# Two attention and MLP layers on one Trainium2 core: the head's loads spread over two queues, and half of layer one's key sum made by GpSimd and VectorE adds

## The chip, the cores and the metric

The kernel runs on one core of a Trainium2 chip. The core has five instruction streams: TensorE (PE in the profile; its weight loads are shown apart as PEld), VectorE (DVE), ScalarE (ACT), GpSimd (POOL) and SyncE (SP), which here only issues DMAs. ScalarE and GpSimd issue DMAs too. Each engine runs its own instructions strictly in the order in which the program gives them; engines wait for one another by semaphores.

The metric is the device time of one execution in microseconds (us); lower is better.

## The reference

Input `x` has 2048 tokens of width 512 in bf16. The same two steps are made twice, with the same weights:

```python
phi = lambda t: jnp.where(t > 0, t + 1, jnp.exp(t)) + 1e-6
# x = x + A(layernorm(x)):   32 heads of width 16
q, k, v = heads(y @ wqkv)
kv  = einsum("bhsd,bhse->bhde", phi(k), v)
z   = einsum("bhsd->bhd", phi(k))            # sum over all 2048 tokens
num = einsum("bhqd,bhde->bhqe", phi(q), kv)
den = einsum("bhqd,bhd->bhq", phi(q), z) + 1e-6
A   = merge(num / den) @ wo
# x = x + B(layernorm(x)):   F = 1792
B   = gelu(y @ w1 + b1) @ w2 + b2
```

So a layer is a linear attention, whose `kv` and `z` need every token of the layer before the first output token can be made, and an MLP. "Layer one" and "layer two" are the two passes. Names in the code have the layer as 0 or 1.

## The kernel before, in words

**Tiles.** The 2048 tokens are 16 tiles of 128 tokens; four tiles are a chunk. A name such as `K0_5` is the K projection of layer one, tile 5; `Q0_1_3` is a Q projection of chunk 1. Matrix products are in bf16 with up to 512 columns at a time.

**Layer one's attention, by tile.** `norm` makes the statistics (`stats`, line 775, and `aggr`, 777, on VectorE), adds eps (`veps`, 782), raises to the power -1/2 on GpSimd (`pow`, 784) and applies the result, on VectorE (803) or, with a further small GpSimd operation `nmr` (795), on ScalarE (798). Tile 3 of chunk 0 has its statistics on ScalarE instead (`sum` 766, `sq` 770). The normalised tile is transposed, by a DMA of SP's queue (`TA0_n`, line 812), or in chunk 0 by TensorE (`PTC0`, `PTC1`, `PTA0_2`, `PTA0_3`, line 825) with a ScalarE copy out of PSUM (`tc...`, line 835). Tiles 0 and 1 of chunk 0 are transposed centred only (`cen`, 789), so that they need not wait for the power; their K projection is scaled afterwards. Then come the K projection (`attn_k`, line 879; K0_0 is written in four parts of the contraction, `K0_0a` to `K0_0d`, in the order given by `ks0`), `phi` (exp on ScalarE 847, relu on ScalarE 858, or a form with max on VectorE 851 and 853, min and add on VectorE 860 and 864, some adds on GpSimd), and the product G = y^T phi(K), which is summed over the tiles in PSUM (`attn_g_held`, line 984). V itself is never made: G is multiplied by its weights later (`KV`, line 1034).

**The sum z.** Layer one makes it by chunks on TensorE: `Z0_c` is 16 matmuls with one output column (line 970), and VectorE adds the result to `zs` (`zs0_c`, 941). Layer two adds phi(K) of chunks 0 to 2 up in `zacc` (fp32, `za...`, line 958, on VectorE or GpSimd), splits the total into two bf16 parts (`zhi` 923, `zlo` 926), sums these over the partitions by eight one-column matmuls (`ZH`, lines 933 and 934) and adds them to `zs` (`zsh`), and makes only chunk 3 as `Z1_3`. From `zs` VectorE builds the block matrix `zb` (1040) for the denominators of chunk 0 (`D0_0_n`, line 1100, then ln and exp on ScalarE) and the diagonal `dz` (1045) for a row of sums (`ZR`, 1048), with which the other chunks' denominators are made token by token on GpSimd and VectorE (1077 to 1089).

**The rest.** After `KV`, `M` and the output projection `WO` (1123) comes the residual add (1128), the second norm, `W1` (1153) with GELU on ScalarE (1158), `W2` (1190) and the residual add (1196, in layer two 1200). The bias b2 is added to `x` ahead of that by a 128 x 512 add in fp32 (`b20_n`, `b21_n`, line 1139) on VectorE or GpSimd. Layer two's norm, K projection and sums follow tile by tile behind layer one's `W2`. The last tile is written in two parts (1176 to 1202).

**What sets the order.** Everything is written down in `CONF`: `LOADS` has the first DMAs with their queue and what they wait for; `ORDER` has every engine's instructions by name, in order; `PLACES` has the buffer slot of each tile and thereby which earlier user must be done; `WAY` says on which engine an operation runs. The code builds a graph of operations, `Settled` takes orders and places from `CONF`, `assign_waits` turns the dependences into semaphore waits, and `play` emits the instructions. There is no planner in the kernel; an operation starts when its engine has finished those ahead of it and its inputs have come.

**The head.** Before the first K projection, TensorE runs 15 warm-up matmuls on constants (line 749). The loads, in their order by queue: SP issues `x0` (tile 0, 128 KB), `x1` (tiles 1 to 3 of chunk 0, 384 KB), `wka`, `wkc` (a quarter of the K weights each, 128 KB), `xc1` (chunk 1, 512 KB, only when `x0` has landed), `wq`, `xc3`, two transposes and `xc2`; ScalarE issues `wkb` and `wkd` as soon as VectorE has set `onesm`. The weights `wv`, `wo`, `w1`, `w2` are loaded from GpSimd's queue later.

The orders around the start, before the change:

```
SP   x0 x1 wka wkc xc1 wq xc3 TA0_0 TA0_1 xc2 TA0_5 TA0_4 ...
ACT  wkb wkd sumA0_3 tcC0 sqA0_3 tcC1 reluk0_0 tcA0_2 expk0_0 tcA0_3 expk0_1 ...
DVE  ones statsA0_0 aggrA0_0 cenA0_0 statsA0_2 statsA0_1 aggrA0_2 aggrA0_1 cenA0_1 normA0_0 vepsA0_1 normA0_2 statsA0_5 normA0_3 ...
PE   warm0 warm8 warm2 warm6 PTC0 warm1 warm7 warm5 warm4 warm3 K0_0a K0_0b PTC1 K0_0c K0_0d PTA0_2 K0_1 PTA0_3 K0_2 K0_3 G0_0_0 ...
PE   ... G0_7_0 Q0_1_1 Z0_3 Q0_0_3 Z0_2 G0_8_0 G0_9_0 D0_0_2 ...
```

The functions that the diff touches, and what calls them:

Of the kernel before, what the change touches and what calls it, by code (L numbers as in the profile page):

```python
# [1359 lines left out]
```

## Time and profile before

| | us |
|---|---|
| median of three runs | 323.17 |
| lowest, highest | 322.78, 323.90 |
| the profiled execution's own time | 323.1 |
| its span in the trace | 321.9 |
| TensorE busy | 318.0 |
| VectorE busy | 218.1 |
| ScalarE busy | 189.3 |
| GpSimd busy | 145.5 |

The profile page gives the busy time of each engine and its number of instructions, then the span in 40 equal slices with the busy share of each slice in tenths. "Chain" is the work that ended last, followed back from the end to what released each step. A group row has line, engine, operation, output and inputs, the number of instructions, then busy time and the mean length of one in ns, then the idle time of that engine just ahead of them and what ended it. A timeline row has start, length, engine, line and operation, and in brackets the idle time ahead of it with its releaser. A windows row has, for a stretch of time, the busy time of PE, PEld, VectorE, ScalarE and GpSimd with their instruction counts, the clock that TensorE was granted (1.00 is full), the mean share in which the 16 DMA engines were busy, and GB/s. Merged rows (x8) run from the start of the first to the end of the last; matmuls overlap, so the length of one row is not its cost on the engine: from start to start a 512-column matmul takes 0.216 us where nothing waits.

### The profile page before, as it was taken

To read this page: it belongs to the slowest core of one execution; us is meant where nothing else is said; L and a number is where in the kernel's file an instruction comes from. 1 tells how busy PE (TensorE), PEld (TensorE's weight loads), DVE (VectorE), ACT (ScalarE), POOL (GpSimd) and SP (SyncE) were. 2 spreads that over 40 slices of the span, in tenths; PEclk is the share of its full clock that TensorE was granted. 3 is DMA by queue.
4 is the path that set the end of the run, shared out by engine and by line. 5 is a ranking of instruction groups with operands and counts; after the bars stand their busy time and mean duration, and the time that the engine had idled before them with its cause. 6 is when DMAs were issued, how large, how long until landed. Compare 5 with 4: busy or idle time off the path is not lost.

```text
span 321.9 us, 4748 instructions
## 1 busy us (share of the span) xinstructions
PE 318.0 (99%) x1703; PEld 157.4 (49%) x1703; DVE 218.1 (68%) x529; ACT 189.3 (59%) x324; POOL 145.5 (45%) x216
## 2 busy tenths in 40 slices
PE   8999999999999999999999999999999999999997
PEld 3444554666444444444444444558544444444444
DVE  5998789999786774028848899999889881101103
ACT  5898656797730636667962367979634442663320
POOL 6573978688655355101822415887454163000000
DMA  7844793142121412111010200122232322201002
GB/s 257 200 81 85 241 348 85 35 82 36 33 49 34 82 33 51 34 33 32 18 40 10 51 16 0 35 51 52 50 62 54 98 65 67 49 0 35 16 33 65
DMA packets 52355, 21.68 MB, mean 67 GB/s; under 512 B 47532, under 2 KB 50860, under 8 KB 52332
## 3 DMA queue, kind: packets, MB, share of 16 engines
q1 hardware_dynamic: 50844, 16.37, 22.4%
q0 software_dynamic: 1056, 4.72, 4.3%
q10 hardware_dynamic: 432, 0.30, 0.3%
q8 instruction: 13, 0.21, 0.3%
q14 instruction: 10, 0.08, 0.1%
HBM read 8.00 MB, written 2.10 MB: 31 GB/s over the span
## 4 chain that ended last, share of the span: by engine, by line
PE 97%; DMA 2%; DVE 0%; issue 0%
PE ps L1153 30%; PE ps L1190 29%; PE ps L1123 9%; PE ps L879 8%; PE ps L896 6%; PE ps L984 4%; PE ps L1013 4%; DMA t<-in_A_x_dram 2%; PE ps L909 2%; PE ps L1176 1%; PE ps L970 1%; PE ps L1034 1%; PE ps L1057 1%; PE ps L1100 1%; DVE stats L775 0%; PE ps L1048 0%
## 5 line engine op out<-in xcount | busy, mean ns | idle before, releaser
L1158 ACT ACTIVATE gT<-ps,b1c 128x512 bf16<-128x512 f32 (+1 forms) x140 | 77.0, 601 | 68.7 <-PE ps L1153 68.1
L1153 PE MATMUL ps<-t,w 128*128 128x512 bf16 (+1 forms) x560 | 102.5, 336 | 0.0
L1190 PE MATMUL ps<-w,gT 128*128 128x512 bf16 x434 | 98.6, 379 | 0.0
L1153 PEld LDWEIGHTS ps<-t,w 128*128 128x128 bf16 x560 | 54.8, 98 | 43.7 <-ACT gT L1158 0.2
L1190 PEld LDWEIGHTS ps<-w,gT 128*128 128x128 bf16 x434 | 42.5, 98 | 50.4
L784 POOL TENSOR_TENSOR rstd<-veps,neghalf 128x1 f32<-128x1 f32 x64 | 39.0, 625 | 41.1 <-DVE veps L782 38.9
L847 ACT ACTIVATE eb<-ps 128x512 bf16<-128x512 f32 x62 | 35.4, 606 | 19.3 <-PE ps L896 7.3
L1200 DVE TENSOR_TENSOR yb<-ps,xsb 128x512 bf16<-128x512 f32 x15 | 10.2, 688 | 41.4 <-PE ps L1190 41.4
L775 DVE BATCH_NORM_STATS2 stats<-xsb 128x6 f32<-128x512 f32 x48 | 32.0, 681 | 0.3
L1123 PE MATMUL ps<-gtb,t 128*128 128x512 bf16 x128 | 31.4, 379 | 0.0
L879 PE MATMUL ps<-wqkv,t 128*128 128x512 bf16 x128 | 30.9, 379 | 0.3 <-ACT t L835 0.3
L858 ACT ACTIVATE rb<-ps 128x512 bf16<-128x512 f32 x43 | 25.3, 607 | 5.8 <-PE ps L879 5.8
L798 ACT ACTIVATE yb<-xsb,nmr,rstd 128x512 bf16<-128x512 f32 x21 | 16.9, 814 | 15.1 <-POOL nmr L795 15.1
L896 PE MATMUL ps<-wqkv,t 128*128 128x512 bf16 x96 | 24.1, 379 | 0.0
L1089 POOL TENSOR_TENSOR t<-t,rr 128x512 bf16<-128x512 bf16 x18 | 19.3, 1072 | 9.0 <-DVE rr L1085 6.4
L782 POOL TENSOR_SCALAR veps<-mv 128x1 f32<-128x1 f32 x35 | 8.2, 236 | 32.7 <-DVE mv L777 31.3
L1196 DVE TENSOR_TENSOR xsb<-ps,xsb 128x512 f32<-128x512 f32 x16 | 10.8, 678 | 17.9 <-PE ps L1190 17.9
L1139 POOL TENSOR_TENSOR xsb<-xsb,b2b 128x512 f32<-128x512 f32 x17 | 21.4, 1267 | 3.0 <-DVE yb L803 2.9
L1077 POOL TENSOR_TENSOR lr<-t,zrow 128x512 f32<-128x512 bf16 x14 | 16.5, 1179 | 7.3 <-ACT zrow L997 4.5
L1123 PEld LDWEIGHTS ps<-gtb,t 128*128 128x128 bf16 x128 | 12.5, 98 | 14.5
L803 DVE TENSOR_SCALAR yb<-xsb,mv,rstd 128x512 bf16<-128x512 f32 x27 | 14.5, 542 | 7.3 <-POOL rstd L784 6.0
L879 PEld LDWEIGHTS ps<-wqkv,t 128*128 128x128 bf16 x128 | 12.1, 98 | 14.7 <-ACT t L835 0.9
(99 smaller groups left out, 363.7 us busy)
## 6 DMA issues: line engine op xcount, KB each, us to landing
w<-in_B_w_dram POOLq DMA_DIRECT2D x4, 896.0 KB, 9.1
out_dram<-yb SPq DMA_DIRECT2D x15, 128.0 KB, 2.0
t<-in_A_x_dram SPq DMA_DIRECT2D x3, 512.0 KB, 4.8
t<-yb SPq DMA_TRANSPOSE x62, 2.5
wqkv<-in_A_wqkv_dram SPq DMA_DIRECT2D x1, 512.0 KB, 5.9
wqkv<-in_A_wqkv_dram POOLq DMA_DIRECT2D x1, 512.0 KB, 4.7
wo<-in_A_wo_dram POOLq DMA_DIRECT2D x1, 512.0 KB, 5.3
t<-in_A_x_dram SPq DMA_DIRECT2D x1, 384.0 KB, 3.3
```

The lines of the kernel that those rows point to most:

```text
L775: G.op("dve", lambda e: e.bn_stats(stats[:, s.slot, :], src()), 620, reads=src_keys, writes=[k + "s"], tiles=[s, *src_tiles], name=f"stats ...
L784: G.op("pool", lambda e: e.tensor_tensor(rstd[:, s.slot:s.slot + 1], veps[:, s.slot:s.slot + 1], neghalf[:], op=ALU.pow), 570, reads=[k + ...
L847: G.op("act", lambda e: e.activation(eb[:, et.slot, :], bank(bt), ACT.Exp, scale=by()), 478, reads=[src_key, *more_keys], writes=[f"e{tag} ...
L858: G.op("act", lambda e: e.activation(rb[:, rt.slot, :], bank(bt), ACT.Relu, scale=by()), 478, reads=[src_key, *more_keys], writes=[f"r{tag ...
L879: ins = e.matmul(bank(b), lhsT=yTa(yT)[:, dt, k * P:(k + 1) * P], rhs=wqkv[:, dt, D:2 * D], start=(i == 0 and n == 0), stop=(i == len(part ...
L896: ins = e.matmul(bank(b), lhsT=yTa(yT)[:, dt, k * P:(k + 1) * P], rhs=wqkv[:, dt, 0:D], start=(dt == 0), stop=(dt == DT - 1))
L1089: lambda e, d=d, tok=tok, heads=heads: e.tensor_tensor(heads(tok()), heads(tok()), rr[:, d.slot, :].unsqueeze(2).broadcast_to([P, H, DH]), ...
L1123: ins = e.matmul(bank(wb), lhsT=yTa(pq)[:, kt, k * P:(k + 1) * P], rhs=gtb[:, kt, :], start=(kt == 0), stop=(kt == DT - 1))
L1139: G.op("pool" if on_pool else "dve", lambda e: e.tensor_tensor(xsb[:, st, :], xsb[:, st, :], b2b[:], op=ALU.add), 1120 if on_pool else 600 ...
L1153: ins = e.matmul(bank(b, n), lhsT=w1[:, dt, ft * P:(ft + 1) * P], rhs=yTa(yT)[:, dt, k0 * P:k1 * P], start=(dt == 0), stop=(dt == DT - 1))
L1158: G.op("act", lambda e, ft=ft, b=b, k0=k0, k1=k1, n=n: e.activation(gT[:, g.slot, ft * 512 + k0 * P:ft * 512 + k1 * P], bank(b, n), ACT.Ge ...
L1190: ins = e.matmul(bank(b), lhsT=gT[:, g.slot, ft * 512 + k * P:ft * 512 + (k + 1) * P], rhs=w2[:, ft, :], start=(ft == 0), stop=(ft == FT - 1))
```

## The change

The change has three parts, and all orders are drawn anew with them.

1. `LOADS`: `x1` goes from the second place on SP's queue to the first on ScalarE's, behind the setting of `onesm`; `wkb` and `wkd` follow it there; `wka` and `wkc` move up on SP. The parts of K0_0 are taken in the order 0, 2, 1, 3.
2. `WAY["zc0"] = "0 1"`: in layer one, phi(K) of the eight tiles of chunks 0 and 1 is added up in `zacc` by seven adds (`zaA1`, `zaA3` to `zaA7` on GpSimd, `zaA2` on VectorE), and `zhiA`, `zloA`, `ZHA` and `zshA` take the total to `zs`, as layer two has it; `Z0_0`, `Z0_1` with their adds `zs0_0`, `zs0_1` go. `Z0_2` and `Z0_3` stay. The code for it was there already, unused in layer one.
3. `ORDER`, `PLACES` and other entries of `WAY` are new: in sum 14 of the b2 adds go from GpSimd to VectorE and two the other way, and some adds and products of layer two and of the denominators change engine.

The order in which chunks are taken (`CHUNKS`) can now be given, but it is 0, 1, 2, 3 in all three places as before; code for loading half a tile and for denominators half by token is added and not used.

```diff
-    LOADS=[['x0', 'sp', 'x', 0, 0, 1, ''], ['x1', 'sp', 'x', 0, 1, 4, ''], ['wkb', 'act', 'wk', 0, 2, 3, 'ones'], ['wka', 'sp', 'wk', 0, 0, 1, ''], ['wkd', 'act', 'wk', 0, 3, 4, ''], ['wkc', 'sp', 'wk', 0, 1, 2, ''], ['xc1', 'sp', 'x', 1, 0, 4, 'x0'], ['wq', 'sp', 'wq', 0, 0, 4, ''], ['xc3', 'sp', 'x', 3, 0, 4, ''], ['xc2', 'sp', 'x', 2, 0, 4, '']],
+    LOADS=[['x0', 'sp', 'x', 0, 0, 1, ''], ['wka', 'sp', 'wk', 0, 0, 1, ''], ['wkc', 'sp', 'wk', 0, 1, 2, ''], ['x1', 'act', 'x', 0, 1, 4, 'ones'], ['wkb', 'act', 'wk', 0, 2, 3, ''], ['wkd', 'act', 'wk', 0, 3, 4, ''], ['xc1', 'sp', 'x', 1, 0, 4, 'x0'], ['wq', 'sp', 'wq', 0, 0, 4, ''], ['xc3', 'sp', 'x', 3, 0, 4, ''], ['xc2', 'sp', 'x', 2, 0, 4, '']],
+    CHUNKS=[[0, 1, 2, 3], [0, 1, 2, 3], [0, 1, 2, 3]],
...
-        "den0_3": "tok", "den1_1": "tok", "den1_2": "tok", "den1_3": "tok", "ks0": "2|0|3|1", "normA0_0": "dve",
+        "den0_3": "tok", "den1_1": "tok", "den1_2": "tok", "den1_3": "tok", "ks0": "0|2|1|3", "normA0_0": "dve",
...
+        "za8": "dve", "za9": "dve", "zaA2": "dve", "zc0": "0 1",
...
-        def attn_z(L, c, pks):
-
-            by_sum = [int(v) for v in (eng("zc0") or "").split()] if L == 0 else list(range(NC - 1))
+        def attn_z(L, c, pks, order):
+
+            by_sum = [int(v) for v in (eng("zc0") or "").split()] if L == 0 else order[:NC - 1]
+            others = [v for v in order if v not in by_sum]
...
-            total(b, f"zc{L}_{c}", f"zs{L}_{c}", bool(L) or c != min(v for v in range(NC) if v not in by_sum))
-            if L == 0 and by_sum and c == max(v for v in range(NC) if v not in by_sum):
+            total(b, f"zc{L}_{c}", f"zs{L}_{c}", bool(L) or c != others[0])
+            if L == 0 and by_sum and c == others[-1]:
                 fold(True)
```

The orders around the places that the change touches, after it:

```
SP   x0 wka wkc xc1 wq xc3 TA0_1 TA0_0 xc2 TA0_4 TA0_7 ...
ACT  x1 wkb wkd sumA0_3 tcC0 sqA0_3 tcC1 expk0_0 tcA0_2 reluk0_0 tcA0_3 expk0_1 ...
DVE  ones statsA0_0 aggrA0_0 cenA0_0 statsA0_2 aggrA0_2 statsA0_1 aggrA0_1 vepsA0_1 cenA0_1 normA0_0 normA0_2 normA0_1 statsA0_4 normA0_3 ...
DVE  ... phik0_15 mink0_10 zhiA mink0_8 phik0_13 phik0_10 mink0_9 mink0_11 phik0_9 phik0_11 zloA zs0_2 zs0_3 zshA zb0 dz0 ...
POOL ... powA0_7 nmrA0_7 zaA1 vepsA0_5 powA0_5 ... powA0_14 nmrA0_15 zaA3 powA0_12 zaA4 nmrA0_14 vepsA0_10 powA0_10 nmrA0_10 vepsA0_8 zaA5 powA0_8 vepsA0_11 nmrA0_8 vepsA0_9 powA0_11 nmrA0_11 powA0_9 zaA6 zaA7 phik0_14 phik0_8 b1z wv wo w1_0 w1_1 ...
PE   warm0 warm7 warm4 warm3 warm6 PTC0 warm1 warm8 warm2 K0_0a warm5 K0_0b K0_0c PTC1 K0_0d PTA0_2 K0_1 PTA0_3 K0_2 K0_3 G0_0_0 ...
PE   ... K0_9 Q0_0_3 G0_7_0 Z0_3 G0_8_0 Z0_2 Q0_1_1 ZHA G0_9_0 D0_0_2 G0_10_0 ZR0 D0_0_0 ...
```

More of the change, by code (lines that the diff above doesn't have):

```diff
@@ L709, in load_w, with load_half @@
                                [f"{which}_{d}" for d in range(d0, d1)], name=name, kb=128 * (d1 - d0), after=after)
+        def load_half(name, queue, h, after):
+            G.parts[("x0", 0)] = (("x0", 0, 0), ("x0", 0, 1))
+            ps_ = slice(64 * h, 64 * h + 64)
+            loaded[name] = dma(queue, lambda e: e.dma_start(
+                t4[ps_, x0[0].slot, 0:D].rearrange("p (k d) -> p k d", k=1), rows(x_dram, 0)[ps_, 0:1, :]),
+                [("x0", 0, h)], [x0[0]], name=name, kb=64, after=after)
         for name, queue, what, at, lo, hi, behind in cf["LOADS"]:
             after = [loaded[b] for b in behind.split()]
-            if what == "x":
+            if what == "half":
+                load_half(name, queue, at, after)
+            elif what == "x":
                 load_x(name, queue, at, lo, hi, after)
@@ L887, in attn_q, with fn @@
         def attn_q(L, c, yT, pq):
-            if by_token(L, c):
-                for k in range(4):
+            half = by_half(L, c)
+            own = pq
+            if half:
+                own = tokq[(L, c)] = Tile(T4, f"pqt{L}_{c}")
+            n = 2 * P if half else 4 * P
+            if not by_token(L, c):
+                for kt in range(DT):
+                    b = Tile(psum, f"q{L}_{c}_{kt}" + "c" * half, "q")
+                    def fn(e, kt=kt, b=b):
+                        for dt in range(DT):
+                            ins = e.matmul(bank(b, n), lhsT=wqkv[:, dt, kt * P:(kt + 1) * P], rhs=yTa(yT)[:, dt, 0:n],
+                                           start=(dt == 0), stop=(dt == DT - 1))
+                        return ins
+                    G.op("pe", fn, 4 * MM if n == D else 4 * (n / 2.4 + 2.5), reads=[f"yT{L}_{4 * c + k}" for k in range(n // P)] + ["wq"], writes=[f"q{L}_{c}_{kt}" + "c" * half],
+                         tiles=[b, yT], name=f"Q{L}_{c}_{kt}" + "c" * half, lat=MM_DRAIN, n=4)
+                    phi(b, f"q{L}_{c}_{kt}" + "c" * half, lambda kt=kt: yTa(pq)[:, kt, 0:n], f"pq{L}_{c}_{kt}" + "c" * half, [pq], f"q{L}_{c}_{kt}" + "c" * half, n=n)
+            for k in range(4):
+                if by_token(L, c, k):
                     b = Tile(psum, f"q{L}_{c}_{k}", "q")
@@ L1042, in attn_kv @@
                  reads=["zs", "bdmask"], writes=["zb"], name=f"zb{L}", lat=40, fast=True)
-            if any(by_token(L, c) for c in range(NC)):
+            if any(by_token(L, c, 3) for c in range(NC)):
                 zr = Tile(psum, f"zr{L}", "t")
@@ new lines, in attn_den @@
+            half = by_half(L, c)
+            src = tokq[(L, c)] if half else pq
+            pt = pq if half or not by_token(L, c) else Tile(T4, f"pt{L}_{c}")
+            n = 2 * P if half else 4 * P
+            if not by_token(L, c):
+                for kt in range(DT):
+                    tag = f"{L}_{c}_{kt}" + "c" * half
+                    b = Tile(psum, f"d{tag}", "n")
+                    r = Tile(LR, f"lr{tag}")
+                    key = f"pq{L}_{c}_{kt}" + "c" * half
+                    G.op("pe", lambda e, kt=kt, b=b: e.matmul(bank(b, n), lhsT=zb[:, kt * P:(kt + 1) * P], rhs=yTa(pq)[:, kt, 0:n], start=True, stop=True),
+                         MM if n == D else n / 2.4 + 2.5, reads=[key, "zb"], writes=[f"d{tag}"], tiles=[b, pq], name=f"D{tag}", lat=MM_DRAIN)
+                    G.op("act", lambda e, b=b, r=r: e.activation(lr[:, r.slot, 0:n], bank(b, n), ACT.Ln, bias=eps6[:]), 575 if n == D else 362,
+                         reads=[f"d{tag}", "eps6"], writes=[f"l{tag}"], tiles=[b, r], name=f"ln{tag}", lat=90, table="exp")
+                    G.op("act", lambda e, r=r: e.activation(lr[:, r.slot, 0:n], lr[:, r.slot, 0:n], ACT.Exp, scale=-1.0), 536 if n == D else 323,
+                         reads=[f"l{tag}"], writes=[f"l{tag}"], tiles=[r], name=f"rec{tag}", lat=110, table="exp")
@@ L1093, in attn_den @@
[L1093 to L1105 removed]
+                         lambda e, kt=kt, r=r: e.tensor_tensor(yTa(pq)[:, kt, 0:n], yTa(pq)[:, kt, 0:n], lr[:, r.slot, 0:n], op=ALU.mult),
@@ new lines, in attn_den, with attn_out @@
+                     1150 if on_pool else 600, reads=[f"rr{tag}", f"pq{tag}"], writes=[f"pq{tag}"], tiles=[d, src],
+                     name=f"pr{tag}", lat=60, fast=not on_pool)
+                dma("sp", lambda e, k=k, tok=tok: e.dma_start_transpose(yTa(pt)[:, :, k * P:(k + 1) * P], tok()), [f"pt{tag}"],
+                    tiles=[src, pt], reads=[f"pq{tag}"], name=f"TP{tag}", sem=("pT", src, k), transpose=True)
+            return pt
+        def attn_out(L, c, k, pq, base, base_keys, base_tiles, first):
@@ L1116, in attn_out @@
             st = 4 * c + k
             wb = Tile(psum, f"wo{L}_{st}", "w")
-            parts = [(kt,) for kt in range(DT)] if st == 0 else [tuple(range(DT))]
+            parts = [(kt,) for kt in range(DT)] if first else [tuple(range(DT))]
             for part in parts:
@@ L1252, in build_kernel @@
         for L in range(2):
-            nxt = []
-            for c in range(NC):
+            nxt = {}
+            chunks = orders[1 + L]
+            for c in chunks:
                 yT = Tile(T4, f"yBT{L}_{c}")
```

155 lines of the change are left out of this document (66 added, 89 removed), and 471 rows, old and new, of tables (ORDER, PLACES, WAY).

## The prediction

> **What bounds the kernel now.** I read the page's busy shares and slices first, then the groups of TensorE (PE), the start of the timeline, and the windows of the stages that the change touches.
>
> ```profile
> span 321.9 us, 4748 instructions
> PE 318.0 (99%) x1703; PEld 157.4 (49%) x1703; DVE 218.1 (68%) x529; ACT 189.3 (59%) x324; POOL 145.5 (45%) x216
> PE   8999999999999999999999999999999999999997
> PE 97%; DMA 2%; DVE 0%; issue 0%
> L879 PE MATMUL ps<-wqkv,t 128*128 128x512 bf16 x128 | 30.9, 379 | 0.3 <-ACT t L835 0.3
> L1153 PE MATMUL ps<-t,w 128*128 128x512 bf16 (+1 forms) x560 | 102.5, 336 | 0.0
> L1190 PE MATMUL ps<-w,gT 128*128 128x512 bf16 x434 | 98.6, 379 | 0.0
> ```
>
> PE is busy in every slice, its work is 97% of the chain that ended last, and its large groups have no idle time before them. So only three things can move the time: how many matmuls there are, the head in which PE still waits, and a new wait. The other engines matter only where they become late for PE.
>
> **The head.** Rows of the timeline, from its start:
>
> ```profile
> 0.79 0.87 SPq L702 DMA_DIRECT2D t<-in_A_x_dram  x2
> 0.83 3.63 PE L749 MATMUL ps<-const-bfloat16-1.0 128*128 128x512 bf16 x10 [0.83 <-PEq L1345]
> 1.48 0.86 ACTq L708 DMA_DIRECT2D wqkv<-in_A_wqkv_dram  x2
> 4.60 0.63 ACT L766 ACTIVATE eb<-t 128x512 bf16<-128x512 bf16 x1 [2.52 <-DMA t<-in_A_x_dram]
> 5.23 0.58 ACT L835 ACTIVATE t<-ps 128x512 bf16<-128x512 bf16 x1
> 5.86 0.60 PE L879 MATMUL ps<-wqkv,t 128*128 128x512 bf16 x2 [0.30 <-ACT t L835]
> 6.73 0.14 DVE L782 TENSOR_SCALAR veps<-mv 128x1 f32<-128x1 f32 x1
> 6.98 0.60 ACT L835 ACTIVATE t<-ps 128x512 bf16<-128x512 bf16 x1 [0.47 <-PE ps L825]
> 7.48 0.68 ACT L858 ACTIVATE rb<-ps,rstd 128x512 bf16<-128x512 f32 x1
> 8.05 0.60 ACT L835 ACTIVATE t<-ps 128x512 bf16<-128x512 bf16 x1
> 8.09 0.69 DVE L775 BATCH_NORM_STATS2 stats<-t 128x6 f32<-128x512 bf16 x1 [0.72 <-DMA t<-in_A_x_dram]
> 8.53 0.70 ACT L847 ACTIVATE eb<-ps,rstd 128x512 bf16<-128x512 f32 x1
> 9.16 0.40 PE L825 MATMUL ps<-idp,yb 128*128 128x128 bf16 x4 [0.47 <-DVE yb L803]
> 9.39 1.89 PE L879 MATMUL ps<-wqkv,t 128*128 128x512 bf16 x8
> 9.59 0.60 ACT L835 ACTIVATE t<-ps 128x512 bf16<-128x512 bf16 x1 [0.37 <-PE ps L825]
> 10.09 0.68 ACT L847 ACTIVATE eb<-ps,rstd 128x512 bf16<-128x512 f32 x1
> 4.00:5.00 1.00, 0.85 (x9) 0.51 (x8) 0.91 (x3) 0.40 (x1) 0.66 (x2) 1.00 1.01 351
> 10.00:30.00 20.00, 20.00 (x122) 9.30 (x121) 18.35 (x60) 18.59 (x35) 11.56 (x30) 1.00 0.51 107
> ```
>
> Tiles 1 to 3 of chunk 0 (x1) have landed at 4.60, and ScalarE's sum of tile 3 starts at once (L766). ScalarE's order puts that sum ahead of the copy of the transposed tile 0 (5.23), which starts K0_0 (5.86). PE's last gap ends at 9.16. The copy of tile 3 at 9.59 lets K0_3 start behind K0_2 in the eight matmuls from 9.39: at 9.39 + 4 x 0.216 = 10.25 (a matmul of 512 columns is 0.216 us behind the one before: 1.89 less the last one's 0.38, over seven). The last two rows are of the windows (PE, weight load, VectorE, ScalarE, GpSimd, granted clock, DMA share, GB/s): the 16 engines of the DMA are full at 351 GB/s, and PE has no gap between 10 and 30 us. What K0_3 loses is lost to the end.
>
> **1. Sums on PE: -0.60 us.** A sum of phi(K) over one chunk is 16 one-column matmuls (L970); the change drops two such groups in layer one and adds ZHA, eight of the kind that layer two has already (L933, L934).
>
> ```profile
> 18.03 0.54 PE L970 MATMUL ps<-onesm,pkb 128*128 128x1 bf16 x16
> 18.43 0.81 PE L984 MATMUL ps<-pkb,yb 128*128 128x512 bf16 x3
> 189.24 0.17 PE L933 MATMUL ps<-onesm,dz 128*128 128x1 bf16 x1
> 189.44 1.89 PE L1013 MATMUL ps<-pkb,yb 128*128 128x512 bf16 x8
> ```
>
> A group costs 18.43 - 18.03 = 0.40, ZH 189.44 - 189.24 = 0.20: 0.20 - 2 x 0.40 = -0.60.
>
> **2. Loads: +0.29 us.** x1 is now the first load of ScalarE's queue, at 1.48 instead of second on SP, which is at 0.79 + 0.87/2 = 1.23: 0.25 later. SP sends wka (128 KB) in the place that x1 had; if its 131 KB go ahead of x1, that is 131/351 = 0.37 us more. Between 0.25 and 0.62, and, if wka and wkc both go first, 0.25 + 0.75 = 1.00. I take 0.45, since the two requests leave the queues a quarter of a microsecond apart and share the engines from then on. The sum of tile 3, the copy of tile 0 and K0_0 move by as much, to 6.31.
>
> Then VectorE's order: the centred tile 1 now stands behind the statistics of both tiles and one more small operation (0.14, the row at 6.73), and the two aggregates no longer run back to back; I take 0.33 of delay, bounds 0.14 and 0.5. The copy of tile 1 starts at 6.98 + 0.45 + 0.33 = 7.76. On ScalarE follow exp, the copy of tile 2, relu and the copy of tile 3, where before one of the two activations came behind it. From start to start the rows give copy 0.50 (6.98 to 7.48), relu 0.57 (7.48 to 8.05), copy 0.48 (8.05 to 8.53), and exp as relu, 0.57: 7.76 + 0.50 + 0.57 + 0.48 + 0.57 = 9.88 for the copy of tile 3. Before it was 9.59, with K0_3 0.66 behind; now K0_3 is at 10.54, +0.29. The other arm, by which chunk 1 lands (8.09), its statistics, tile 3's normalisation and its transpose (9.16), stays as it is: the same bytes are ahead of chunk 1, and one VectorE statistic (tile 4 for tile 5) is still ahead of the normalisation. So the term is not under 0, unless chunk 1 lands earlier too (-0.14, where ScalarE would have let K0_3 go without any delay of x1: 10.54 - 0.45 = 10.09 against 10.25). At x1 late by 1.00 it is +0.84.
>
> wkb and wkd go out behind x1; the last of them is wanted by K0_0d, right ahead of K0_1, which waits for the copy of tile 1 until about 8.4. The new part order of K0_0 (0, 2, 1, 3 for 2, 0, 3, 1) follows the new order of landing and is covered by the same copy. The fifteen warm-up matmuls are the same; one more of them lies ahead of the first transpose, under the 0.6 us that the copy waits anyway.
>
> **3. The denominator's start: +0.26 us.** ZHA gives zs, zs gives zb (VectorE), zb lets D0_0_2 (L1100) go. Before:
>
> ```profile
> 36.91 1.89 PE L984 MATMUL ps<-pkb,yb 128*128 128x512 bf16 x8
> 37.08 0.36 DVE L941 TENSOR_TENSOR zs<-ps,zs 128x4 f32<-128x4 f32 x2 [0.77 <-PE ps L970]
> 37.48 0.69 DVE L1040 TENSOR_TENSOR zb<-bdmask,zs 128x512 bf16<-128x512 bf16 x1
> 38.63 0.38 PE L1100 MATMUL ps<-t,zb 128*128 128x512 bf16 x1
> ```
>
> The last sum matmul started 0.03 before the G products, at 36.88; two adds and zb took until 38.17, and D0_0_2 came at 38.63, behind two G products: 0.46 to spare. Now one G product (4 x 0.216 = 0.86) stands between ZHA and D0_0_2. From the last matmul of ZHA: 0.16 for its result (the length of the L934 kind's row of 189.24), 0.04, 0.20 for the single add, 0.04, 0.69 for zb, about 1.15; PE comes after 0.03 + 0.86 = 0.89. Stall 0.26. With the two adds' time it is 1.29 - 0.89 = 0.40; if the G product is held up itself, nothing: 0 to 0.4.
>
> **4. Adds: 0, up to +2.3.** The eight tiles of phi(K) become seven adds into zacc, six on GpSimd and one on VectorE, then a copy and a subtraction on VectorE.
>
> ```profile
> L958 POOL TENSOR_TENSOR zacc<-zacc,pkb x4: 1156/1158/1337, 157.5 to 179.4; 128x512 f32<-128x512 f32 x4
> L923 DVE TENSOR_SCALAR dz<-zacc x1: 421/421/421, 183.4 to 183.4; 128x512 bf16<-128x512 f32 x1
> L926 DVE TENSOR_TENSOR eb<-zacc,dz x1: 684/684/684, 185.6 to 185.6; 128x512 bf16<-128x512 f32 x1
> 31.42 1.15 POOL L864 TENSOR_TENSOR pkb<-eb,rb 128x512 bf16<-128x512 bf16 x1 [4.94 <-DVE eb L860]
> L1139 POOL TENSOR_TENSOR xsb<-xsb,b2b x17: 1149/1159/1681, 70.3 to 266.4; 128x512 f32<-128x512 f32 x17
> L1139 DVE TENSOR_TENSOR xsb<-xsb,b2b x15: 672/684/1370, 79.3 to 277.2; 128x512 f32<-128x512 f32 x15
> L1034 PE MATMUL ps<-gtb,wqkv x32: 219/219/219, 46.6 to 203.0; 128*128 128x128 bf16 x32
> ```
>
> Six adds of 1.158 are 6.95 us. GpSimd has 11.56 of 20 us busy from 10 to 30, so 18.5 of 20, and it stood idle for 4.94 us before its phi(K) at 31.42. The powers and means of the norms of chunks 2 and 3 stand in order behind the adds; followed through by these durations the last power ends near 28.4 and its tile is transposed by 32.1, when PE wants it. Cover: that 4.94 us. If it is gone, each late add delays all K projections behind it by 1.16. VectorE gets 0.69 + 0.42 + 0.68 + 0.2 less two adds of 0.18, some +1.6, in a stretch in which it was busy 18.35 of 20; its remaining 1.65 us are the cover, and zloA and zb come at its end.
>
> **5. The rest: 0.** The weight loads on GpSimd's queue now go out behind both of its phi(K) products (the one at 31.42 and the next) instead of between them; the first of them, Wv, is needed only at 46.6 (L1034). Sixteen b2 adds change engine, 14 to VectorE (0.684 each, 1.16 on GpSimd); they are done any time before their residual add, and VectorE has 32% free over the span. What stands behind one of them in order waits 0.68 at most, if that cover is missing.
>
> **Sum.** The profiled execution took 323.1 (1.2 beside its span of 321.9; the median of three is 323.17, 322.78 to 323.9): 323.1 - 0.60 + 0.29 + 0.26 + 0 = 323.05, say 323.1. Its own range, by the ends of terms 2 and 3, is 322.5 to 323.7. Some 0.3%, 1 us, is what a measurement of this kernel can tell from no change.
>
> **Rivals.** (a) Slower: GpSimd becomes late in layer one. It decides once the last power ends later than 28.4. For it: 18.5 of 20 us, and the same adds on it took up to 1.681 where VectorE's took up to 1.370 against 0.684, so the two engines stretch each other at times. With all six adds at 1.681 GpSimd's stretch holds 11.56 + 10.1 = 21.6 of 20 us: 1.6 late, 324.7. One add late gives 324.3, two 325.4. Against it: most of its operations there are small and wait for VectorE anyway. The Trainium skill ("SBUF — State Buffer", Who interferes with whom) says that the port pair which VectorE and GpSimd share is an exclusive lock, held for a whole instruction; by that rule the stretched rows are the cost to expect, and it speaks against moving adds to GpSimd beside a busy VectorE. The maxima of the L1139 rows agree, the medians do not.
>
> (b) Slower: VectorE's extra b2 adds make PE's later tiles late, one or two by 0.7 to 1.4 us: 324.0 to 324.5. Against it: PE's 0.0 idle at L1153 and L1190.
>
> (c) Slower: PE idles longer in the head, its clock drops again. The ten first warm-ups (4352 columns by their order) took 3.63 us, half the 0.216 us per 512 later; some 3 us at that rate cost 1.5: 324.6. Against it: the gaps in the rows are under 0.5 us.
>
> (d) Faster: the load order costs nothing, chunk 1 lands earlier, and zb is in time: 323.1 - 0.60 - 0.14 = 322.4, and under 322.2 if the two VectorE steps that now wait for x1 alone close 0.2 more of the head.
>
> (e) The load move does nothing either way and zb stalls: 322.8. The Trainium skill ("DMA: Bandwidth & Descriptors", Issuing engines are not separate DMA queues) has it that queues of different engines share the same DMA engines, so a second queue saves issue time but brings no bandwidth; the full 351 GB/s agrees.
>
> **How the numbers follow.** Forecast 0.48 (0.44 of it within 0.3%), a 0.23, b 0.09, c 0.05, d 0.11, e 0.04. Faster by over 0.3% means under 322.2: d and 0.02 of the forecast, 0.13. Slower means over 324.1: a, b, c and 0.02 of the forecast, 0.39. Same is the rest and e, 0.48. The range from 322.2 to 325.6 leaves out the bottom of d and the top of a.
>
> **What would show it.** Step 1: 48 matmuls at L970's place and 16 of the ZH kind, one-column time down 0.6 us. Step 2: the copy of tile 0 at about 5.7, K0_3 at about 10.5. Step 3: D0_0_2 with 0.26 us of idle PE before it. Step 4: no idle PE at the K projections from 25 to 35 us. The prediction is wrong if PE shows gaps behind GpSimd's powers, or a gap over 0.5 us after 45 us.

## The result, and the profile after

The changed kernel takes 325.5 us (median of six executions, 325.19 to 326.7); the kernel before, beside it, 323.62 (322.78 to 324.5). The ratio is 1.0067, 95% interval 1.0049 to 1.0086: slower by 2.2 us by the ratio, by 1.9 us by the medians. The profiled execution took 325.34 with a span of 324.1, against 323.1 and 321.9, so its 2.2 us can be looked up row by row.

The page of the changed kernel; line numbers are shifted against before (879 is 895, 970 is 991, 958 is 979, 864 is 880):

```profile
span 324.1 us, 4706 instructions
PE 319.0 (98%) x1679; PEld 156.4 (48%) x1679; DVE 228.8 (71%) x551; ACT 191.9 (59%) x326; POOL 137.4 (42%) x202
PE 89%; DVE 4%; ACT 2%; POOL 2%; DMA 1%; issue 1%; DVEq 0%; ACTq 0%; POOLq 0%
L895 PE MATMUL ps<-wqkv,t 128*128 128x512 bf16 x128 | 32.4, 380 | 2.1 <-ACT rb L874 0.6
```

PE's share of the chain fell from 97% to 89%: VectorE, ScalarE and GpSimd now appear in it. The one large group with idle time ahead of it is the K projections, 2.1 us for 0.3. PE's rows of the timeline there:

```profile
25.31 0.59 PE L895 MATMUL ps<-wqkv,t 128*128 128x512 bf16 x2
26.09 1.90 PE L895 MATMUL ps<-wqkv,t 128*128 128x512 bf16 x8 [0.19 <-ACT eb L863]
27.83 1.03 PE L1005 MATMUL ps<-pkb,yb 128*128 128x512 bf16 x4
29.17 1.04 PE L895 MATMUL ps<-wqkv,t 128*128 128x512 bf16 x4 [0.32 <-DVE t L869]
30.80 1.04 PE L895 MATMUL ps<-wqkv,t 128*128 128x512 bf16 x4 [0.59 <-ACT rb L874]
32.10 2.65 PE L895 MATMUL ps<-wqkv,t 128*128 128x512 bf16 x10 [0.27 <-DVE pkb L869]
```

The loss is the distance of a start from the start that 0.216 us per matmul would give, a little more than the idle time in brackets. Two matmuls from 25.31 end their turn at 25.74, the next start is 26.09: 0.35 (K0_12). In the same way 27.83 + 0.86 against 29.17 is 0.48 (K0_14), 0.76 at 30.80 (K0_10), 0.44 at 32.10 (K0_8), and the last row is 0.31 longer than ten matmuls need (K0_11). Together 2.34 us. Each waits for a PSUM bank whose earlier contents ScalarE or VectorE has not yet read: layer one's K and Q products have four banks, the other four hold G.

Why those two are late shows on GpSimd and ScalarE:

```profile
20.47 1.15 POOL L979 TENSOR_TENSOR zacc<-zacc,pkb 128x512 f32<-128x512 f32 x1
23.97 1.16 POOL L979 TENSOR_TENSOR zacc<-zacc,pkb 128x512 f32<-128x512 f32 x1
25.09 0.83 POOL L800 TENSOR_TENSOR rstd<-veps,neghalf 128x1 f32<-128x1 f32 x1
26.29 0.44 POOL L811 TENSOR_SCALAR nmr<-mv,rstd 128x1 f32<-128x1 f32 x1
28.06 0.37 POOL L811 TENSOR_SCALAR nmr<-mv,rstd 128x1 f32<-128x1 f32 x1
28.92 2.38 POOL L979 TENSOR_TENSOR zacc<-zacc,pkb 128x512 f32<-128x512 f32 x2
```

```profile
23.65 0.81 ACT L814 ACTIVATE yb<-t,nmr,rstd 128x512 bf16<-128x512 bf16 x1 [0.29 <-POOL nmr L811]
25.44 0.60 ACT L863 ACTIVATE eb<-ps 128x512 bf16<-128x512 f32 x1
26.76 0.81 ACT L814 ACTIVATE yb<-t,nmr,rstd 128x512 bf16<-128x512 bf16 x1 [0.72 <-POOL nmr L811]
27.48 0.58 ACT L863 ACTIVATE eb<-ps 128x512 bf16<-128x512 f32 x1
28.47 0.81 ACT L814 ACTIVATE yb<-t,nmr,rstd 128x512 bf16<-128x512 bf16 x1 [0.41 <-POOL nmr L811]
30.14 0.60 ACT L874 ACTIVATE rb<-ps 128x512 bf16<-128x512 f32 x1
```

K0_12 waits for the exp at 25.44. ScalarE was late for it from 23.65 on, where the norm of tile 10 waited 0.29 us for its `nmr`; that stands on GpSimd behind the adds zaA3 (18.66 to 19.81) and zaA4 (20.47). The add zaA5 (23.97) stands ahead of the power and `nmr` of tile 8 (26.29). ScalarE's norm of tile 8 waits for that until 26.76, and the exps and relus behind it in ScalarE's order, which would free PE's banks, wait too. Next come the norm of tile 11, late by 0.41, and the relu at 30.14 that K0_10 waits for.

VectorE has its own delay, first in the changed kernel, then the row of the kernel before for the last of these norms:

```profile
18.88 0.68 DVE L791 BATCH_NORM_STATS2 stats<-t 128x6 f32<-128x512 bf16 x1
24.02 1.38 DVE L880 TENSOR_TENSOR t<-eb,rb 128x512 bf16<-128x512 bf16 x1
26.80 0.41 DVE L880 TENSOR_TENSOR pkb<-eb,rb 128x512 bf16<-128x512 bf16 x1
28.42 0.69 DVE L869 SCALAR_TENSOR_TENSOR t<-ps,eb 128x512 bf16<-128x512 f32 x1
30.14 1.31 DVE L819 TENSOR_SCALAR yb<-t,mv,rstd 128x512 bf16<-128x512 bf16 x1
31.37 0.68 DVE L869 SCALAR_TENSOR_TENSOR pkb<-ps,eb 128x512 bf16<-128x512 f32 x1
```

```profile
26.26 0.41 DVE L803 TENSOR_SCALAR yb<-t,mv,rstd 128x512 bf16<-128x512 bf16 x1
```

The same operation takes 1.38 us beside the add of 23.97 to 25.13, and 0.41 at 26.80, where GpSimd runs nothing wide. The norm at 30.14, 0.41 in the kernel before, takes 1.31 beside the last add, and K0_8 at 32.10 waits for the phi(K) operation right behind it on VectorE (31.37). The statistics at 18.88 keep their 0.68 beside zaA3.

The rest of the balance: D0_0_2 waits 0.26, and W11_0_11_0 at 217.35 waits 0.19 (behind eight matmuls from 215.43). The head gives 0.07 back (K0_3 at 10.19 for 10.26), the sums -0.60. So 2.34 + 0.26 + 0.19 - 0.07 - 0.60 = 2.1 of 2.2 us.

### The profile page after: what moved, and what is told of

Its sections match the earlier page's. It is cut to its first block, busy times and chain, and to the rows that moved or that the text cites. A ratio compares the mean times of both kernels' runs of the same rounds, so it can differ in the third digit from the quotient of the medians.

```text
span 324.1 us, 4706 instructions
## 1 busy us (share of the span) xinstructions
PE 319.0 (98%) x1679; PEld 156.4 (48%) x1679; DVE 228.8 (71%) x551; ACT 191.9 (59%) x326; POOL 137.4 (42%) x202
## 4 chain that ended last, share of the span: by engine, by line
PE 89%; DVE 4%; ACT 2%; POOL 2%; DMA 1%; issue 1%; DVEq 0%; ACTq 0%; POOLq 0%
PE ps L1179 30%; PE ps L1216 29%; PE ps L1149 9%; PE ps L928 6%; PE ps L895 5%; PE ps L1034 4%; PE ps L1005 2%; PE ps L916 1%; DVE stats L791 1%; DMA t<-in_A_x_dram 1%; PE ps L1202 1%; DVE yb L819 1%; ACT eb L863 1%; POOL rstd L800 1%; ACT t L851 1%
## 5 line engine op out<-in xcount | busy, mean ns | idle before, releaser
L800 POOL TENSOR_TENSOR rstd<-veps,neghalf 128x1 f32<-128x1 f32 x64 | 40.1, 635 | 38.6 <-DVE veps L798 35.3
L895 PE MATMUL ps<-wqkv,t 128*128 128x512 bf16 x128 | 32.4, 380 | 2.1 <-ACT rb L874 0.6
L798 POOL TENSOR_SCALAR veps<-mv 128x1 f32<-128x1 f32 x30 | 7.5, 249 | 42.8 <-DVE mv L793 41.1
L928 PE MATMUL ps<-wqkv,t 128*128 128x512 bf16 x96 | 24.3, 379 | 0.0
L1165 DVE TENSOR_TENSOR xsb<-xsb,b2b 128x512 f32<-128x512 f32 x27 | 20.1, 758 | 3.5 <-ACT yb L814 3.5
L1120 POOL TENSOR_TENSOR lr<-t,zrow 128x512 f32<-128x512 bf16 x14 | 17.2, 1232 | 7.1 <-ACT zrow L1018 4.0
```

What stands on the lines that cost most here:

```text
L800: G.op("pool", lambda e: e.tensor_tensor(rstd[:, s.slot:s.slot + 1], veps[:, s.slot:s.slot + 1], neghalf[:], op=ALU.pow), 570, reads=[k + ...
L895: ins = e.matmul(bank(b), lhsT=yTa(yT)[:, dt, k * P:(k + 1) * P], rhs=wqkv[:, dt, D:2 * D], start=(i == 0 and n == 0), stop=(i == len(part ...
L928: ins = e.matmul(bank(b), lhsT=yTa(yT)[:, dt, k * P:(k + 1) * P], rhs=wqkv[:, dt, 0:D], start=(dt == 0), stop=(dt == DT - 1))
L1165: G.op("pool" if on_pool else "dve", lambda e: e.tensor_tensor(xsb[:, st, :], xsb[:, st, :], b2b[:], op=ALU.add), 1120 if on_pool else 600 ...
```

## The experiments

Three theories were put against each other. A: the adds hold GpSimd, and what stands behind them in its order makes ScalarE late. B: an add stops VectorE's operations while it runs. C: the adds are innocent, and the newly drawn orders and bank places are too tight. Later a theory D on the loads was added. In the diffs `moved(engine, names, behind)`, `dropped` and `place` edit the strings of `ORDER` and `PLACES`.

**Narrow adds.**

```diff
-                             zacc[:], pkb[:, p0.slot, :] if fresh else zacc[:], pkb[:, pks[k].slot, :], op=ALU.add),
+                             zacc[:, 0:w], pkb[:, p0.slot, 0:w] if fresh else zacc[:, 0:w], pkb[:, pks[k].slot, 0:w], op=ALU.add),
+   # w = 16 for zaA3 to zaA7, else D
```

> The changed kernel with the five GpSimd adds zaA3 to zaA7 made on 16 of the 512 columns (so the sum z of chunks 0 and 1 is left incomplete), every order and place as in the changed kernel. Theory A (the full adds hold GpSimd, and the small operations for ScalarE's norms stand behind them in order) and theory B (the full adds stop VectorE's operations while they run) both expect the gaps of PE at the K projections between 25 and 35 us, 2.3 us together in the changed kernel, to fall under 0.5 us, and the time to about 323.2 to 323.6. Theory C (the adds are innocent: the newly drawn orders and bank places are too tight in themselves) expects the gaps to stay above 1.8 us and the time at about 325.4.

324.13 us against 323.18: ratio 1.0023 (1.0009 to 1.0038). The windows of 24 to 34 us of the kernel before, the changed kernel, and this one (columns: PE, PEld, VectorE, ScalarE, GpSimd busy, clock, DMA share, GB/s):

```profile
24.00:34.00 10.00, 10.00 (x62) 4.76 (x61) 8.44 (x24) 8.39 (x16) 4.77 (x10) 1.00 0.36 73
```

```profile
24.00:34.00 10.00, 8.50 (x37) 3.04 (x36) 8.55 (x21) 7.94 (x15) 7.41 (x11) 1.00 0.33 66
```

```profile
24.00:34.00 10.00, 10.00 (x48) 4.58 (x47) 9.00 (x26) 9.66 (x20) 5.21 (x11) 1.00 0.34 70
```

PE goes from 8.50 back to 10.00 busy with every order and place as in the changed kernel. C falls: nothing in the new orders is too tight at the K projections by itself. The time is still 0.5 us above the 323.2 to 323.6 that was expected. In the profiled execution what is lost lies in the head: G0_0_0, the first product behind the first K projections, starts at 11.91, where it started at 11.12 before. The loads experiments take this up.

**GpSimd held as long, with hardly any data.**

```diff
+                    def hold(e):
+                        e.tensor_tensor(idle[:, 0:1], onesm[:, 0:1], neghalf[:], op=ALU.pow)
+                        return e.tensor_tensor(idle[:, 1:2], onesm[:, 0:1], neghalf[:], op=ALU.pow)
-                         lambda e, k=k, ...: e.tensor_tensor(zacc...
+                         hold if L == 0 and st > 2 else lambda e, k=k, ...: e.tensor_tensor(zacc...
```

> The changed kernel with each of the adds zaA3 to zaA7 replaced by two GpSimd powers on one column (0.55 us each, about 1.1 us together, so z of chunks 0 and 1 is left incomplete): GpSimd is held as long as by an add, but moves almost no data. Theory A expects the gaps of PE at the K projections to stay near 2 us and the time near 325.2. Theory B expects VectorE's two stretched operations (1.38 and 1.31 us where others of the kind take 0.41) to go back to about 0.41, the gaps to fall under 0.8 us and the time to about 323.5. If both have a share, the gaps lie between, near 1.2 us.

324.19 us, ratio 1.0033 (1.0017 to 1.0048). The same window:

```profile
24.00:34.00 10.00, 9.50 (x44) 3.95 (x43) 8.15 (x22) 9.16 (x18) 7.66 (x15) 1.00 0.33 67
```

GpSimd is as busy as in the changed kernel (7.66 for 7.41), PE loses a third as much. From start to start the gaps are 0.41 (K0_14) and 0.42 (K0_10), 0.83 together, where the changed kernel has 2.34. (A further 0.11 at 15.93 lies ahead of the first held add, at 19.20.) The two stretched operations of VectorE are gone:

```profile
24.25 0.41 DVE L881 TENSOR_TENSOR t<-eb,rb 128x512 bf16<-128x512 bf16 x1
29.78 0.41 DVE L820 TENSOR_SCALAR yb<-t,mv,rstd 128x512 bf16<-128x512 bf16 x1
```

Both theories hold a part: some 0.8 us come from GpSimd's order alone, the other 1.5 need adds that move data.

**The adds behind the last power.**

```diff
+moved("pool", ["zaA3", "zaA4", "zaA5", "zaA6", "zaA7"], "powA0_9")
```

> The changed kernel with zaA3 to zaA7 moved on GpSimd behind the last power of layer one's norms (powA0_9); nothing is left out. Theory A expects ScalarE's norms of tiles 14, 10, 8 and 11 on time, PE's gaps at the K projections under 0.6 us and the time about 323.4. Theory B expects five adds in a row from about 26 to 32 us, VectorE operations stretched beside them by 0.3 to 1 us each, gaps of 1 us or more in PE after 28 us, and about 324.5. Theory C expects about 325.4.

326.33 us, ratio 1.0091 (1.0074 to 1.0108): slower than the changed kernel. ScalarE's norms hardly wait (0.18 at most), and the gaps at K0_12, K0_14 and K0_10 are gone. In their place K0_9 waits 1.85 us, for a PSUM bank that VectorE's phi(K) operation has not yet read; K0_8 and K0_11 wait as before, 0.35 and 0.31. The adds now stand in one row beside VectorE:

```profile
28.51 1.31 DVE L837 TENSOR_SCALAR yb<-t,mv,rstd 128x512 bf16<-128x512 bf16 x1
29.74 0.68 DVE L887 SCALAR_TENSOR_TENSOR pkb<-ps,eb 128x512 bf16<-128x512 f32 x1
30.34 0.84 DVE L898 TENSOR_TENSOR t<-eb,rb 128x512 bf16<-128x512 bf16 x1
31.11 1.24 DVE L885 TENSOR_SCALAR eb<-eb 128x512 bf16<-128x512 bf16 x1
```

These are the gaps that B expects after 28 us; the time is 1.8 us above the 324.5 that was expected from them. Some 1.5 us are lost after 55 us, at an output projection behind VectorE (0.57) and in the MLP (0.83 and 0.10, behind a GELU); what made these late was not followed up.

**The sums back on PE.** The second part undone, in the changed orders; the tiles and places had to be put somewhere.

```diff
+CONF["WAY"]["zc0"] = ""
+moved("pe", ["Z0_0"], "G0_3_0")
+moved("pe", ["Z0_1"], "K0_9")
+place("psum_5", "k0_5", "zc0_0 k0_5")
+place("psum_5", "zc0_2", "zc0_1 zc0_2")
...
```

> The changed kernel with its second part undone: chunks 0 and 1 are summed by Z0_0 and Z0_1 on PE again, no adds, no ZHA; loads, order of everything else and the b2 adds as changed. Theories A and B expect 325.4 - 2.3 (gaps) - 0.26 (the wait of D0_0_2) + 0.60 (24 one-column matmuls) = about 323.4. Theory C expects the gaps to stay and 325.6 or more.

326.3 us, ratio 1.009 (1.0075 to 1.0105): neither theory's number. Of the gaps of the changed kernel only 0.20 at K0_10 is left, but the places chosen for the sums make new ones: 0.40 at K0_5, which now waits for a bank that a sum holds, and 0.88 ahead of Z0_1, which waits for phi(K) of a later tile. Behind that the MLP loses another 1.5 us, 0.96 of it at 81.45, behind a GELU. The run says that most of the gaps at the K projections go with the adds; as a price of the second part it is of no use.

**The fold alone, in the kernel before.** Adds where GpSimd stood idle.

```diff
+CONF["WAY"]["zc0"] = "0 1"
+# pool: ... powA0_4 zaA1 ...   nmrA0_11 zaA3 zaA4 zaA5 zaA6 zaA7
+# dve:  zaA2 for zs0_0;  mink0_8 zhiA;  zloA zs0_2 zs0_3 zshA
+# pe:   G0_8_0 ZHA G0_9_0 G0_10_0 D0_0_2
```

> The kernel before with the sums of chunks 0 and 1 by adds alone: zaA1 on GpSimd early, zaA2 on VectorE, zaA3 to zaA7 on GpSimd behind its last small operation (26.5 us, where it stood idle 4.9 us), ZHA in, D0_0_2 behind two G products as before; loads and b2 adds as before. Theory A alone (small operations behind the adds) expects no loss, since none stands behind them: 323.2 - 0.6 = 322.6. Theory B (adds stop VectorE's operations from SBUF to SBUF) expects VectorE operations of over 0.8 us between 26 and 33 us, PE gaps of 1 us or more there, and 323.6 to 324.6.

329.03 us, ratio 1.0173 (1.015 to 1.0196). A falls as the whole story: nothing small stands behind these adds. The five adds run in one row on GpSimd, and beside them VectorE:

```profile
27.18 6.51 POOL L986 TENSOR_TENSOR zacc<-zacc,pkb 128x512 f32<-128x512 f32 x5
```

```profile
27.40 1.38 DVE L892 TENSOR_TENSOR t<-eb,rb 128x512 bf16<-128x512 bf16 x1
28.70 1.24 DVE L879 TENSOR_SCALAR eb<-eb 128x512 bf16<-128x512 bf16 x1
29.98 0.69 DVE L881 SCALAR_TENSOR_TENSOR t<-ps,eb 128x512 bf16<-128x512 f32 x1
31.30 1.37 DVE L892 TENSOR_TENSOR t<-eb,rb 128x512 bf16<-128x512 bf16 x1
32.59 1.24 DVE L879 TENSOR_SCALAR eb<-eb 128x512 bf16<-128x512 bf16 x1
```

Four operations that take 0.29 or 0.41 alone take 1.24 to 1.38, 0.95 to 0.97 us more each, 3.8 together; the one at 29.98, which reads PSUM, takes its usual 0.69. Of the 5.9 us, 3.2 are lost at K0_15 (1.33), K0_9 (1.29) and K0_11 (0.59), each waiting for VectorE, whose order runs through these rows. The rest is not shown to be B's. Z0_2 waits 1.49 us for a phi(K) that GpSimd makes behind its adds and behind two weight loads, the first of which it issued only after 1.93 us in which the profile shows nothing that it waited for. And K0_6 waits 1.23 us at 22.49, before these five adds begin, for its transposed tile; why that came late was not followed up.

**Adds in halves.**

```diff
+                    def halves(e, k=k):
+                        for h in (slice(0, 256), slice(256, 512)):
+                            ins = e.tensor_tensor(zacc[:, h], zacc[:, h], pkb[:, pks[k].slot, h], op=ALU.add)
+                        return ins
```

> The changed kernel with each of zaA3 to zaA7 made as two adds of 256 columns, one after the other; nothing is left out. GpSimd is held as long (0.1 to 0.4 us more in all), so theory A expects the gaps as they are or larger, 325.4 to 325.8. Theory B expects a VectorE operation to wait for half an add at most, so none over 0.9 us beside them, the gaps at the K projections to shrink from 2.3 to 1.2 us or so, and 324.4.

326.02 us, ratio 1.0082 (1.0062 to 1.0103). Beside the adds no VectorE operation takes over 0.89 us, as B expects, yet the gaps stay: 0.51 + 0.82 + 0.43 + 0.42 = 2.2 us. Two halves take 1.29 to 1.48 us where one add takes 1.15 to 1.19, up to 0.3 us more for every operation behind them in GpSimd's order. That what VectorE won was lost there fits these rows, but was not tested by itself. K0_0 also started late in this profile (6.72), behind an x1 that landed at 5.46.

**D0_0_2 one product later.**

```diff
+moved("pe", ["D0_0_2"], "G0_10_0")
```

> The changed kernel with D0_0_2 moved behind G0_10_0 on PE, so that two G products stand between ZHA and it as before: the gap of 0.26 us before it should go and the span fall by about 0.2 us, if the ScalarE operation behind it does not become late; the gaps at the K projections stay.

The gap ahead of D0_0_2 is gone: eight matmuls from 41.28 (one of them left no record) end their turn at 43.01 and it starts at 43.00. But the single execution took 327.63, with a span of 326.4. Most of this is in its head, where the clock that PE was granted fell:

```profile
6.00:7.00 1.00, 0.06 (x1) 0.06 (x2) 0.97 (x3) 1.00 (x4) 0.43 (x2) 1.00 0.89 321
7.00:8.00 1.00, 1.00 (x4) 0.40 (x5) 0.93 (x5) 0.59 (x2) 0.92 (x3) 0.64 1.05 349
8.00:9.00 1.00, 1.00 (x7) 0.60 (x6) 1.00 (x4) 0.21 (x1) 0.83 (x3) 0.50 1.08 423
9.00:10.00 1.00, 1.00 (x7) 0.62 (x6) 0.72 (x2) 1.00 (x3) 0.26 (x2) 0.50 0.47 190
```

PE stood idle for 1.4 us ahead of K0_0a (6.94), since x1 had landed only at 5.68; then the clock is 0.50 up to 10.7. The narrow adds had the same late x1 (5.61) and a full clock, and there K0_0a started at 6.87 and G0_0_0 at 11.91, here at 6.94 and 12.87: the clock cost about 0.9 us. Against the changed kernel G0_0_0 is 1.8 us late; another 0.7 us are lost between 50 and 72 us, which was not followed up, so one execution can't tell what the new place of D0_0_2 is worth.

**The loads alone, in the kernel before.**

```diff
+# LOADS of the changed kernel
+dropped("sp", ["x1"])
+CONF["ORDER"]["act"] = "x1 " + CONF["ORDER"]["act"]
```

> The kernel before with the new loads alone: x1 first on ScalarE's queue, wkb and wkd behind it, wka and wkc up on SP; every other order as before. In the kernels run so far with these loads K0_0 started between 6.0 and 6.9 us (5.86 before). Theory D (the move of x1 makes the head uncertain and late by 0.1 to 0.8 us) expects PE to lose 0.1 to 0.8 us up to K0_3 and nothing behind it: 323.3 to 324.0. The rival (the load move is free) expects 323.2 and K0_3 at 10.25 or sooner.

324.17 us, ratio 1.0028 (1.0012 to 1.0045). x1 landed at 6.17, K0_3 started at 11.33.

**The loads put back, in the changed kernel.**

```diff
+# LOADS of the kernel before
+CONF["ORDER"]["sp"] = CONF["ORDER"]["sp"].replace("x0 wka", "x0 x1 wka")
+dropped("act", ["x1"])
```

> The changed kernel with the loads of the kernel before (x1 second on SP, wkb and wkd alone on ScalarE's queue); the rest as changed. By the loads theory (x1 on ScalarE's queue lands anywhere from 4.8 to 6.2 us, on SP at 4.6) x1 lands at 4.6 and K0_3 starts at about 10.0, and the median falls by about 0.6 to 0.9 us, to 324.6 to 324.9; the gaps at the K projections stay at 2.3 us. If the loads had no share, 325.5.

325.62 us, ratio 1.0065 (1.0044 to 1.0087), as the changed kernel: nothing is got back, although x1 landed at 4.62 in the profile and K0_3 started at 10.04. The two runs contradict each other, so two more put the loads where the adds cost nothing, and together with the part order that belongs to them.

> The changed kernel with zaA3 to zaA7 on 16 columns (z of chunks 0 and 1 left incomplete) and the loads put back. With the narrow adds alone the median was 324.1 (before 323.2). If the load move has a share of its own, as the before-kernel with the new loads alone suggested (0.9 us more), this falls to 323.0 to 323.4; if x1 lands late at times in either load order and the move has no share, it stays at 323.9 to 324.3.

323.72 us, ratio 1.0008 (0.9993 to 1.0023): between the two expectations.

```diff
-"ks0": "2|0|3|1"
+"ks0": "0|2|1|3"
```

> The kernel before with the new loads and with the new order of K0_0's four parts (0, 2, 1, 3), which follows them. If the load move has a share of its own, 323.8 to 324.3 again, 0.6 us or more over the kernel before; if the 0.9 us of the loads alone came from the old part order, which starts with the weights that now land late, or from chance, 323.0 to 323.4.

323.12 us, ratio 0.9994 (0.9981 to 1.0007): the new loads with the new part order cost nothing that can be measured. What the profiles show is that x1's landing varies with either order. ScalarE's first row of the head, where it waits for x1, in the changed kernel, in the kernel with narrow adds (both with x1 on ScalarE's queue), and in the mixed kernel below (x1 on SP):

```profile
4.76 0.63 ACT L782 ACTIVATE eb<-t 128x512 bf16<-128x512 bf16 x1 [2.67 <-DMA t<-in_A_x_dram]
```

```profile
5.61 0.63 ACT L782 ACTIVATE eb<-t 128x512 bf16<-128x512 bf16 x1 [3.52 <-DMA t<-in_A_x_dram]
```

```profile
5.65 0.63 ACT L807 ACTIVATE eb<-t 128x512 bf16<-128x512 bf16 x1 [3.56 <-DMA t<-in_A_x_dram]
```

Over all profiles x1 landed at 4.76 to 6.17 on ScalarE's queue (nine profiles, five of them after 5.0) and at 4.60 to 5.75 on SP's (six, three after 5.0). Whether the move has a small share of its own stays open: it is not seen beside this variation, and the 0.9 us of the loads alone may be the old part order, which begins with weights that now go out behind x1, or chance; that one profile had the latest x1 of all.

**Adds on VectorE.** With the loads put back, zaA3 to zaA7, and then only zaA5 to zaA7, on VectorE.

```diff
+CONF["WAY"].update({f"zaA{i}": "dve" for i in (3, 4, 5, 6, 7)})
+moved("dve", ["zaA3"], "phiq0_0_1")
+moved("dve", ["zaA4"], "normA0_12")
+moved("dve", ["zaA5"], "statsA0_9")
+moved("dve", ["zaA6"], "phiq0_0_2")
+moved("dve", ["zaA7"], "phiq0_1_2")
```

> The kernel with the loads put back, and in addition zaA3 to zaA7 on VectorE (0.68 each), each behind an operation after which its tile of phi(K) is there. No full add is left on GpSimd but zaA1, so theory A and theory B both expect nothing of GpSimd: no VectorE operation over 0.8 us before 30 us, ScalarE's norms on time. VectorE gets 3.4 us more work between 19 and 30 us, where it was busy without the stretches some 8.5 of 10: gaps of about 1 to 2 us in PE from that, 323.8 to 324.8. If VectorE has no room at all, 325 or more.

325.37 us, ratio 1.007 (1.0042 to 1.0098). No single VectorE operation took over 0.69 us from 16 to 30 us, but VectorE is full (5.00 of 5 us busy from 20 to 25 and from 25 to 30), and PE waits 0.63, 0.45 and 0.84 at K0_12, K0_14 and K0_10. Its profiled execution, 326.74, had the late x1 and the clock of 0.50 from 7 to 10 us as well.

```diff
+CONF["WAY"].update({f"zaA{i}": "dve" for i in (5, 6, 7)})
+moved("dve", ["zaA5"], "phiq0_0_2")
+moved("dve", ["zaA6", "zaA7"], "phiq0_1_2")
```

> The kernel with the loads put back, zaA3 and zaA4 on GpSimd as changed, and zaA5 to zaA7 on VectorE, behind its operations at 27.1 and 29.1 us, where it stood idle 0.5 and 0.7 us. Theory A keeps the delay of two adds for ScalarE's norms of tiles 14 and 10, but not of 8 and 11; theory B loses the two long stretches (1.38 and 1.31 us). Gaps of 0.5 to 1.2 us at the K projections, 323.4 to 324.0: the best that these pieces give, near the kernel before and not clearly under it.

324.29 us, ratio 1.0038 (1.0024 to 1.0053): the best whole kernel with the adds. It gets back half of the loss, and the kernel before stays ahead. The gaps at the K projections are 0.24, 0.26, 0.72 and 0.25, 1.5 us.

## Why the prediction was wrong, point by point

**The step that failed is 4, "Adds: 0, up to +2.3".** It entered the sum as 0; the profile has 2.34 us there. Three things were wrong in it. The cover was an average: the 4.94 us in which GpSimd stood idle lie at 26.5 to 31.4, behind its last small operation, while zaA3 to zaA5 stand at 18.7 to 25.1 among operations that follow at once. The follower was wrong: I followed the last power to its transposed tile, and that one was no problem (it ended at 28.95 for 28.4, and K0_9 was not late for it); late were the `nmr` values for ScalarE's norms, with ScalarE's exps queued behind them and PE's banks behind those. And VectorE was counted as if it ran at its usual speed beside GpSimd. The held GpSimd shows the first two at about 0.8 us; the other 1.5 need the adds' data. The measured 325.5 lies just inside the stated range, whose upper end came from rival (a); the forecast itself, no change that could be told from noise, did not come true.

**Rival (a) is what happened**, at its price of two late adds (325.4). That the price fits is luck: it stands for two adds of 1.16 us handed on to PE in full, where the runs show 0.8 us from GpSimd's order and 1.5 from stretched VectorE operations. It had the point of decision (the last power later than 28.4) about right by accident. It also looked for the stretch on the wrong engine: the `zacc` adds of both layers on GpSimd hardly grew (median 1.154, 1.534 at most), VectorE's operations did. The rule of the Trainium skill ("SBUF — State Buffer", Who interferes with whom) quoted there, an exclusive lock held for a whole instruction, agrees with the rows of the fold alone: 1.24 to 1.38 for operations that take 0.29 to 0.41, each until the add beside it is over. I weighed it by medians over all b2 adds, which hide it: most VectorE operations that start beside one read PSUM, or are statistics, row sums or small reciprocals, and keep their times. Single rows of the profile before have it. Beside the b2 add that took 1.681, a VectorE operation of 0.29 takes 1.25:

```profile
153.05 1.68 POOL L1139 TENSOR_TENSOR xsb<-xsb,b2b 128x512 f32<-128x512 f32 x1
```

```profile
153.63 1.25 DVE L860 TENSOR_SCALAR eb<-eb 128x512 bf16<-128x512 bf16 x1
```

**Step 1, -0.60**, was right: 0.40 for a group and 0.21 for ZHA in the new profile, and the narrow adds lose nothing between 24 and 34 us.

**Step 3, +0.26**, was right to the row:

```profile
39.45 0.16 PE L955 MATMUL ps<-onesm,eb 128*128 128x1 bf16 x1
39.48 1.02 PE L1005 MATMUL ps<-pkb,yb 128*128 128x512 bf16 x4
40.60 0.39 PE L1094 MATMUL ps<-t,zb 128*128 128x512 bf16 x1
```

D0_0_2 could start at 39.48 + 0.86 = 40.34 and starts at 40.60; moved one product later, its gap is gone.

**Step 2, +0.29**, was wrong in its form. In the profiled execution x1 was 0.16 late, not 0.45, and K0_3 came 0.07 earlier than before. Over the profiles with a full clock K0_3 starts from 0.3 us earlier to 1.1 later than before with x1 on ScalarE's queue, and from 0.2 earlier to 0.85 later with x1 on SP's: what I took for a price of the move varies as much with either order of the loads. The copy of tile 0 behind the sum of tile 3 in ScalarE's order, which I named, is what hands a late x1 on to PE.

**Step 5, 0**, missed 0.19 at W11_0_11_0. **Rival (b)** (VectorE's b2 adds) shows nothing else in PE's rows of the changed kernel. **Rival (c)**, the clock, is not in the changed kernel's profile but in two of the experiments: PE idle for 1.4 and 1.7 us ahead of K0_0a, then 0.50 for some 3.4 us. Its price, 1.5 us estimated, was about 0.9 in the one where it could be read. **Rivals (d) and (e)** did not happen; that the load move does little either way, as (e) has it, fits the load runs.

## What to carry to other kernels

An idle engine is cover only at the place in its order where the new work stands: list what follows the new instruction on its queue, and who waits for that, before its idle time is counted. Price wide GpSimd operations with what they do to VectorE: here each one cost a VectorE operation between SBUF tiles up to 1 us. And 0.6 us less on a full TensorE is worth nothing if its four free PSUM banks are emptied by the two engines that pay for it.
